# Cosformer attention and a token-mixing MLP on one core: tile-scheduled batches against a fixed order of head-pair slots

## The chip, the core and the metric

One NeuronCore of a Trainium2 chip runs the kernel; the other seven cores are idle. The metric is device time in microseconds. Before the change it was 181.37 us (median of three runs, 178.93 to 183.41). One more execution was profiled: its own time was 179.77 us, and its span from the first to the last recorded instruction 178.0 us.

## What is computed

There are 8 batches, 8 heads, 576 positions and 64 features a head. Float32 goes in and out; the kernel computes in bfloat16 with float32 sums.

```python
def phi(x, c, s):                      # c, s: cos and sin of pi/2 * pos/576
    r = np.maximum(x, 0.0)
    return np.concatenate([r * c, r * s], axis=-1)      # 64 -> 128 features
kv  = np.einsum('bhsf,bhsd->bhfd', phi(k), v)           # 128 x 64 for each head
z   = np.sum(phi(k), axis=2)
num = np.einsum('bhsf,bhfd->bhsd', phi(q), kv)
den = np.einsum('bhsf,bhf->bhs', phi(q), z)[..., None] + 1e-06
x   = num / den                                         # heads side by side: 576 x 512
W   = 1/8 * (x @ w_q) @ (x @ w_k).T                     # 576 x 576, never formed
out = np.maximum(W @ x, 0.0) @ w_out
```

Both kernels use W @ x = (x @ w_q) @ ((x @ w_k).T @ x): a 64 x 512 product "kx", then "mix" = relu(1/8 kx.T (x w_q).T), then mix times w_out.

## The kernel before, in words

The unit of work is a head pair: two heads, whose 2 x 576 x 64 values of q, k or v lie in memory as 128 partitions x 576 numbers. Partitions 0 to 63 hold the first head and 64 to 127 the second; 9 chunks of 64 features lie in each partition. Four pairs make a batch.

The loop at L278 goes over the batches. `attention` (L112) loads q, k and v on the SP queue in halves of a batch (quarters for batch 0). Relu of k and q (L140, ScalarE nearly always) goes to bfloat16, and VectorE multiplies each by a table of cos and sin (L142) into k_p and q_p, twice as wide. GpSimd casts v (L135) into a buffer in which each head has its own 65 columns (64 and a column of ones, for z) and zeros in the other head's columns, so that one 128-row matmul with 130 columns serves both heads. For each pair, TensorE forms kv_ps (L153, 9 matmuls) and transposes q_p (L163, 9); kv_ps and qpt_ps are copied to SBUF (L161, L167); then 5 matmuls a head give numerator and denominator (L175), and VectorE takes the reciprocal (L183) and multiplies (L184) into x_sb.

`moe_front` (L191) transposes x (L196, copied at L201), forms (x w_q).T and (x w_k).T in one product (L207, copied at L214), transposes the second back (L218, L225), forms kx (L229, L237) and mix (L242, L249). `wout` (L256) runs once for two batches: 9 row tiles of 4 matmuls (L260), a copy each (L268), two stores each on the SP queue (L276).

Nothing fixes the order by hand: the tile framework's scheduler interleaves the batches by dependencies and priorities, and `nc.any` lets it choose between VectorE and ScalarE. At the start 26 warming matmuls run (L60), tables and zeroed buffers are made, and the weights are loaded on ScalarE's queue.

PSUM has 8 banks: one each for kv_ps, 2 for qpt_ps, 2 for num_ps, 3 shared by everything of the mlp (tag "moe").

## Time and profile before

| | |
|---|---|
| runs: median (range) | 181.37 us (178.93 to 183.41) |
| profiled execution: its own time, its span | 179.77 us, 178.0 us |
| TensorE matmul busy in the span | 147.2 us (83%) |
| VectorE busy | 134.1 us (75%) |
| ScalarE, GpSimd busy | 89.9 us, 56.6 us |
| granted TensorE clock, mean | 0.932 |
| HBM read, written | 29.62 MB, 9.44 MB |

PE is TensorE, PEld its weight loads, DVE VectorE, ACT ScalarE, POOL GpSimd, SP the engine that issues transfers. A row "128x65 bf16 x320 | 21.3, 196" says 320 instructions of that shape, 21.3 us together, 196 ns of one on average. The end of a matmul is modelled and its time holds a fixed latency, so consecutive matmuls overlap in the records: what TensorE really spends on one is the spacing of starts in a run of equals.

### The profile page before, as it was taken

The page shows a single profiled execution, that of the slowest core. Times are in us where ns is not written, and L with a number is a line of the kernel's source. Part 1 is how long each engine was busy: PE and PEld are TensorE (multiplying, and loading weights), DVE is VectorE, ACT ScalarE, POOL GpSimd, SP SyncE. Part 2 cuts the span into 40 slices and gives each one's busy share as a digit, 9 for nine tenths or more (in the row PEclk, how much of TensorE's full clock was granted, in tenths as well). Part 3 has the DMA queues.
Part 4 walks back from the last instruction along what each step waited for, and adds up shares of the span by engine and source line. Part 5 has one row for each costly group of instructions (what it writes and reads, how often), then busy time and mean ns, then how long its engine had stood idle before and what let it go on. Part 6 is the DMA issues. An engine that isn't in the chain of part 4 may idle for free.

```text
span 178.0 us, 3706 instructions
## 1 busy us (share of the span) xinstructions
PE 147.2 (83%) x1434; PEld 90.6 (51%) x1434; DVE 134.1 (75%) x279; ACT 89.9 (51%) x167; POOL 56.6 (32%) x75
## 2 busy tenths in 40 slices
PE   6920776889958999999989999998999999759930
PEld 2300774656645446875745467675544756423410
DVE  5827989869999899897799999879994976722000
ACT  3028155148607869525496862491885426033630
POOL 8636283887882300000576000145800000000000
PEclk9995579579999999999999999999999999996996
DMA  6999999999792038789990587999008850000886
GB/s 172 312 393 315 382 397 392 391 392 388 256 387 109 2 80 186 166 220 398 397 385 37 130 204 170 292 400 389 19 0 195 205 135 0 4 0 0 189 201 140
DMA packets 20513, 39.30 MB, mean 221 GB/s; under 512 B 3088, under 2 KB 3088, under 8 KB 20496
## 3 DMA queue, kind: packets, MB, share of 16 engines
q1 hardware_dynamic: 18912, 37.76, 66.7%
q10 hardware_dynamic: 1584, 1.31, 2.5%
q8 instruction: 11, 0.18, 0.4%
q14 instruction: 6, 0.05, 0.1%
HBM read 29.62 MB, written 9.44 MB: 219 GB/s over the span
## 4 chain that ended last, share of the span: by engine, by line
PE 56%; DVE 17%; ACT 10%; DMA 8%; issue 4%; SPq 1%; POOL 0%; ACTq 0%
PE moe_ps_e L260 10%; PE kv_ps L153 10%; PE qpt_ps L163 9%; PE moe_ps_d L242 6%; PE moe_ps_c L229 5%; PE xT_ps L196 5%; PE num_ps L175 5%; DMA qf<-in_q_dram 5%; DVE k_p L142 5%; PE moe_ps_a L207 4%; DVE q_p L142 3%; DVE qpt_sb L167 3%; DVE x_sb L184 3%; ACT wqkT_sb L214 2%; DMA wq_f<-in_moe_w_q_dram 2%
## 5 line engine op out<-in xcount | busy, mean ns | idle before, releaser
L135 POOL CAST v_buf<-vf 64x576 bf16<-64x576 f32 x64 | 51.2, 822 | 71.9 <-DMA vf<-in_v_dram 33.4
L163 PE MATMUL qpt_ps<-ident,q_p 128*128 128x128 bf16 x288 | 29.8, 228 | 10.5 <-DVE q_p L142 9.4
L260 PE MATMUL moe_ps_e<-wo_sb,mix_sb 128*128 128x512 bf16 x144 | 33.9, 391 | 0.3
L153 PE MATMUL kv_ps<-v_buf,k_p 128*128 128x130 bf16 x288 | 29.0, 235 | 2.0 <-ACT kv_sb L161 0.8
L184 DVE TENSOR_TENSOR x_sb<-num_ps,rec 128x320 bf16<-128x320 f32 x64 | 29.8, 481 | 0.1
L167 DVE COPY qpt_sb<-qpt_ps 128x1152 bf16<-128x1152 bf16 x32 | 24.1, 754 | 4.7 <-PE qpt_ps L163 4.2
L268 ACT COPY o_sb<-moe_ps_e 128x512 f32<-128x512 f32 x34 | 19.9, 586 | 13.5 <-PE moe_ps_e L260 7.2
L163 PEld LDWEIGHTS <-q_p 128*128 128x128 bf16 x288 | 19.1, 102 | 14.9 <-DVE q_p L142 10.7
L175 PE MATMUL num_ps<-kv_sb,qpt_sb 128*128 128x65 bf16 x320 | 21.3, 196 | 3.0 <-DVE x_sb L184 1.5
L142 DVE TENSOR_TENSOR k_p<-rk,cossin 128x2304 bf16<-128x2304 bf16 (+1 forms) x18 | 23.3, 1297 | 0.2 <-ACT rk L140 0.2
L140 ACT ACTIVATE rk<-kf 128x1152 bf16<-128x1152 f32 (+1 forms) x17 | 17.7, 1048 | 11.1 <-DVE k_p L142 5.6
L142 DVE TENSOR_TENSOR q_p<-rq,cossin 128x2304 bf16<-128x2304 bf16 (+1 forms) x18 | 23.2, 1290 | 0.0
L260 PEld LDWEIGHTS <-mix_sb 128*128 128x128 bf16 x144 | 14.1, 100 | 17.0 <-issue 2.6
L153 PEld LDWEIGHTS <-k_p 128*128 128x128 bf16 x288 | 19.7, 105 | 5.3 <-ACT kv_sb L161 1.7
L249 ACT ACTIVATE mix_sb<-moe_ps_d 128x512 bf16<-128x512 f32 (+1 forms) x50 | 19.3, 441 | 5.1 <-PE moe_ps_d L242 4.7
L161 ACT CAST kv_sb<-kv_ps 128x130 bf16<-128x130 f32 x24 | 6.4, 268 | 28.0 <-PE kv_ps L153 28.0
L175 PEld LDWEIGHTS <-qpt_sb 128*128 128x128 bf16 x320 | 15.6, 99 | 9.4 <-issue 2.5
L140 ACT ACTIVATE rq<-qf 128x1152 bf16<-128x1152 f32 (+1 forms) x17 | 18.3, 1080 | 3.4 <-DMA qf<-in_q_dram 3.0
L196 PE MATMUL xT_ps<-ident,x_sb 128*128 128x128 bf16 (+1 forms) x160 | 17.4, 220 | 1.3 <-DVE x_sb L184 1.1
L242 PE MATMUL moe_ps_d<-wqkT_sb,kx_sb 64*128 64x512 bf16 x64 | 14.9, 288 | 1.1 <-ACT kx_sb L237 0.7
L201 DVE COPY xT_sb<-xT_ps 128x576 bf16<-128x576 bf16 x32 | 13.4, 441 | 2.4 <-PE xT_ps L196 2.2
L196 PEld LDWEIGHTS <-x_sb 128*128 128x128 bf16 (+1 forms) x160 | 11.6, 99 | 5.1 <-DVE x_sb L184 1.2
(45 smaller groups left out, 103.0 us busy)
## 6 DMA issues: line engine op xcount, KB each, us to landing
out_dram<-o_sb SPq DMA_DIRECT2D x72, 128.0 KB, 2.4
kf<-in_k_dram SPq DMA_DIRECT2D x14, 576.0 KB, 9.5
vf<-in_v_dram SPq DMA_DIRECT2D x14, 576.0 KB, 9.5
qf<-in_q_dram SPq DMA_DIRECT2D x14, 576.0 KB, 10.5
kf<-in_k_dram SPq DMA_DIRECT2D x4, 288.0 KB, 5.4
vf<-in_v_dram SPq DMA_DIRECT2D x4, 288.0 KB, 6.2
qf<-in_q_dram SPq DMA_DIRECT2D x4, 288.0 KB, 7.5
wo_f<-in_moe_w_out_dram ACTq DMA_DIRECT2D x1, 1024.0 KB, 10.7
```

The source lines that it names most:

```text
L135: nc.gpsimd.tensor_copy(v_ext[p0:p0 + 64, pr, :, hh, 0:D], dst[p0:p0 + 64, pr, :].rearrange("p (c d) -> p c d", c=C9))
L140: nc.any.tensor_scalar(rr[:, a:bb, :, :], dst[:, a:bb, :], 0.0, None, op0=ALU.max)
L142: nc.vector.tensor_mul(pp[:, a:bb, :, :, :], rr[:, a:bb, :, :].unsqueeze(3).to_broadcast([P, step, C9, 2, D]), csb)
L153: nc.tensor.matmul(kv_ps, k_p[:, pr, c, :, :], v_ext[:, pr, c, :, :], start=(c == 0), stop=(c == C9 - 1),)
L163: nc.tensor.transpose(qpt_ps[:, c, :], q_p[:, pr, c, :, :], ident)
L167: nc.vector.tensor_copy(qpt_sb, qpt_ps.rearrange("f c (hh pp) -> f hh c pp", hh=2))
L175: nc.tensor.matmul(num_ps[:, u, :], qpt_sb[:, hh, cb:cb + 2, :], kv_sb[:, hh, :], start=True, stop=True,)
L184: nc.vector.tensor_tensor(x_sb[:, :, h, :], num_ps[:, :, 0:D], rec.to_broadcast([P, SC, D]), op=ALU.mult,)
L196: nc.tensor.transpose(xT_ps[:, j0:j0 + npn], x_sb[p0:p0 + npn, u, 2 * hp:2 * hp + 2, :], ident[p0:p0 + npn, p0:p0 + npn],)
L242: nc.tensor.matmul(mx_ps[:, 0:nn], kx_sb[:, dmc * P:(dmc + 1) * P], wqkT_sb[0:64, n0:n0 + nn], start=True, stop=True,)
L260: nc.tensor.matmul(o_ps, mix_sb[:, dmc, rt * P:(rt + 1) * P], wo_sb[:, dmc, :], start=(dmc == 0), stop=(dmc == NDM - 1),)
L268: nc.any.tensor_copy(o_sb, o_ps)
```

## The change

The whole kernel function is rewritten. The order of the instructions of each engine is now the order of the program text (`manual_schedule`), and the work is cut into 32 slots, one for each head pair g. What is done in a slot:

- `qk_pe(g)`: k'v and the transposed q for one pair. Each head is now a matmul of its own on 64 rows, the two heads alternating; v needs no zero columns. q is only rectified and doubled beforehand (`dup_q`, GpSimd); cos and sin are multiplied in when VectorE evacuates the transposed q (`cst`). Both results share one two-bank tile with one buffer.
- `num(g-1)`: both heads of the pair before, with the 1e-06 added by a small matmul, one reciprocal and one multiplication for both heads, one two-bank buffer.
- Pieces of the mlp of past batches, by r = g mod 4: mix of two batches back (r = 0 and 1), w_out of three batches back, x transposes, x w_k and x w_q, kx. x w_k is computed with x as the stationary operand, so that it needs no transposing back; w_q is stored twice, so that mix's matmuls run on two halves of 64 rows. All these share one PSUM tag of two two-bank buffers, and ScalarE evacuates all of them.
- Preparation: GpSimd alone does relu of k, the cast of v and the doubled relu of q for a pair of head pairs (H), two H ahead; VectorE multiplies k by cos and sin for one H ahead in every odd slot. Loads come three H ahead, in pairs of head pairs.

What does not fit the slots comes after the last slot. The weights are loaded on the SP queue behind the first loads, and cast on ScalarE in slots 1 to 3; 16 warming matmuls are left.

The diff, cut to its core (all lines are of the new kernel):

```diff
+    inp = ctx.enter_context(tc.tile_pool(name="inp", bufs=4))
+    prep = ctx.enter_context(tc.tile_pool(name="prep", bufs=2))
...
+    ctx.enter_context(tc.manual_schedule())
+    def m2_tile(dtype, name):
+        return psum.tile([P, 2, 512 if dtype is FP32 else 1024], dtype,
+                         name=name, tag="m2", bufs=2)
...
+    def load(H, nsplit=1, names=("k", "q", "v")):
...
+                nc.sync.dma_start(raw[nm, H][:, lo:lo + step, :],
+                                  srcs[nm][b][:, h0 + lo:h0 + lo + step, :])
...
+    def relu_k(H, lo, hi, eng):
...
+            eng.tensor_scalar(o, raw["k", H][:, lo:hi, :], FMAX, 0.0,
+                              op0=ALU.min, op1=ALU.max)
+    def mul_k(H, lo, hi):
...
+        nc.vector.tensor_mul(
+            kp[H][:, lo:hi],
+            rks[H][:, lo:hi].unsqueeze(3).to_broadcast([P, n, C9, 2, D]),
+            cossin.unsqueeze(1).to_broadcast([P, n, C9, 2, D]))
+    def cast_v(H, lo, hi, eng):
...
+            eng.tensor_scalar(dst, src, 1.0, 1.0, op0=ALU.mult, op1=ALU.mult)
+    def dup_q(H, lo, hi, eng):
...
+            eng.tensor_scalar(dst, src, FMAX, 0.0, op0=ALU.min, op1=ALU.max)
+    def qk_pe(g):
+        H, i = divmod(g, 2)
+        qk_ps = psum.tile([P, 2, 2048], mybir.dt.uint8, name="qk_ps", bufs=1)
...
+        for c in range(C9):
+            for hh in range(2):
+                p0 = hh * 64
+                nc.tensor.matmul(
+                    kvp[:, hh, :], kp[H][p0:p0 + 64, i, c, :, :],
+                    v_bufs[H % 3][p0:p0 + 64, i, c, 0:D + 1],
+                    start=(c == 0), stop=(c == C9 - 1))
+        for c in range(C9):
+            for hh in range(2):
+                p0 = hh * 64
+                nc.tensor.transpose(
+                    qt[:, hh, c * D:(c + 1) * D],
+                    qd[H][p0:p0 + 64, i, c, :, :],
+                    ident[p0:p0 + 64, p0:p0 + 64])
...
+        nc.vector.tensor_copy(kv_sb, kvp)
+        nc.vector.tensor_mul(
+            qpt_bufs[g % 3][:, :, 1:SLOTS, :],
+            qt.rearrange("f h (c d) -> f h c d", c=C9),
+            cst.unsqueeze(1).to_broadcast([P, 2, C9, D]))
+    def num(g):
...
+        num_ps = psum.tile([P, 2, 512], FP32, name="num_ps", bufs=1)
...
+            for u in range(SC):
+                nc.tensor.matmul(
+                    nv[:, hh, u, :], qpt_bufs[g % 3][:, hh, 2 * u:2 * u + 2, :],
+                    kvs[g][:, hh, :], start=(u == 0), stop=False)
+            nc.tensor.matmul(nv[:, hh, :, D], ones_t, eps_t, start=False, stop=True)
+        nc.vector.reciprocal(rec, nv[:, :, :, D:D + 1])
+        nc.vector.tensor_tensor(
+            xs[b][:, :, 2 * pr:2 * pr + 2, :].rearrange("p u h d -> p h u d"),
+            nv[:, :, :, 0:D], rec.to_broadcast([P, 2, SC, D]), op=ALU.mult)
+    def xT(H, eng):
...
+    def wk_stage(b, eng):
...
+    def wq_stage(b, eng):
...
+    def kx_stage(b, eng):
...
+    def mx(b, st, eng):
...
+            nc.scalar.activation(dst, mx_ps[:, :, 0:hs], AF.Relu, scale=scale_moe)
+    def wout(bp, rt0, n, engs):
...
+            copy(engs[0], o_sb[:, 0:n, :], o_ps[:, 0:n, :])
...
+                nc.sync.dma_start(dst, o_sb[hi * 64:hi * 64 + 64, r, :])
+    A, V, G = nc.scalar, nc.vector, nc.gpsimd
+    load(1)
+    load_w()
+    for lo in range(2):
+        relu_k(0, lo, lo + 1, A)
+        cast_v(0, lo, lo + 1, G)
+        dup_q(0, lo, lo + 1, A if lo == 0 else G)
+        mul_k(0, lo, lo + 1)
+    load(2)
+    relu_k(1, 0, 2, G)
+    cast_v(1, 0, 2, G)
+    dup_q(1, 0, 2, G)
...
+    for g in range(NG):
+        Bc, r = divmod(g, NPAIR)
+        H = g // 2
+        if g % 2 == 0 and H + 3 < NB:
+            load(H + 3)
+        if r == 0 and Bc >= 2:
+            mx(Bc - 2, 0, A)
+        if r == 1 and Bc >= 2:
+            mx(Bc - 2, 2, A)
+        qk_pe(g)
+        if r == 0 and Bc >= 2:
+            mx(Bc - 2, 1, A)
+        if r == 1 and Bc >= 2:
+            mx(Bc - 2, 3, A)
+        if g >= 1:
+            num(g - 1)
+        if g % 2 == 1 and H + 1 < NB:
+            mul_k(H + 1, 0, 2)
...
+        if g % 2 == 0 and H + 2 < NB:
+            relu_k(H + 2, 0, 2, G)
+            cast_v(H + 2, 0, 2, G)
+            dup_q(H + 2, 0, 2, G)
+        if r == 0 and Bc >= 3:
+            wout(*wouts(Bc - 3)[0], (A,))
+        if r == 1:
+            if Bc >= 1:
+                xT(2 * (Bc - 1) + 1, A)
+            if Bc >= 3:
+                wout(*wouts(Bc - 3)[1], (A,))
+        if r == 2:
+            if Bc >= 1:
+                wk_stage(Bc - 1, A)
+                wq_stage(Bc - 1, A)
+            if Bc >= 3 and len(wouts(Bc - 3)) > 2:
+                wout(*wouts(Bc - 3)[2], (A,))
+        if r == 3:
+            if Bc >= 1:
+                kx_stage(Bc - 1, A)
+            xT(2 * Bc, A)
+    num(NG - 1)
+    for st in range(4):
+        mx(B - 2, st, A if st % 2 else V)
+    xT(2 * (B - 1) + 1, V)
+    for w in wouts(B - 3):
+        wout(*w, (A,))
+    wk_stage(B - 1, V)
+    wq_stage(B - 1, A)
+    for w in wouts(B - 2)[:1]:
+        wout(*w, (A,))
+    kx_stage(B - 1, V)
+    for w in wouts(B - 2)[1:]:
+        wout(*w, (A,))
+    for st in range(4):
+        mx(B - 1, st, A if st % 2 else V)
+    for w in wouts(B - 1):
+        wout(*w, (A, V))
```

`xT` makes 10 transposes of 128 x 128 and one copy of 128 x 1152; `wk_stage` 20 matmuls of 64 columns and a copy of 128 x 640; `wq_stage` 8 matmuls of 288 columns and a copy of 128 x 576; `kx_stage` 5 matmuls of 512 columns and a copy of 128 x 512; each `mx` 2 matmuls of 288 columns, each on 64 rows of its own, and a copy of 128 x 576; `wout` 4 matmuls of 512 columns for a row tile and one copy for two tiles. In this diff H counts pairs of head pairs (two slots), g head pairs, b batches; `wouts(b)` gives 2 or 3 groups of at most two row tiles.

More of the change, by code (lines that the diff above doesn't have):

```diff
@@ L56, with warm_up @@
+    load(0, nsplit=2)
     warm = consts.tile([P, 512], BF16)
     nc.vector.memset(warm, 1.0)
[L58 to L60 removed]
+    warm_ps = m2_tile(FP32, "warm_ps")
+    def warm_up(n):
+        for _ in range(n):
+            nc.tensor.matmul(warm_ps[:, 0, :], warm[:, 0:P], warm,
+                             start=True, stop=True)
+    warm_up(16)
@@ new lines, in xT, with copy @@
+    def xT(H, eng):
+        b, h = divmod(H, 2)
+        xT_ps = m2_tile(BF16, "xT_ps")
+        for i in range(2):
+            hp = 2 * h + i
+            for u in range(SC):
+                nc.tensor.transpose(
+                    xT_ps[:, i, u * P:(u + 1) * P],
+                    xs[b][:, u, 2 * hp:2 * hp + 2, :], ident)
+        copy(eng, xT_bufs[b % 2][:, 2 * h:2 * h + 2, D:SLOTS * D],
+             xT_ps[:, :, D:SLOTS * D])
+    def copy(eng, dst, src):
+        if eng is nc.scalar:
+            nc.scalar.copy(dst, src)
+        else:
+            eng.tensor_copy(dst, src)
@@ L256, in wout @@
-    def wout(b0, mix_sb):
-        for rt in range(2 * S // P):
-            o_ps = psum.tile([P, DM], FP32, name="moe_ps_e", tag="moe", bufs=3)
+                    wk_ps[:, 0, u * DH:(u + 1) * DH],
+                    xT_bufs[b % 2][:, dmc, u * P:(u + 1) * P],
+                    wk_sb[:, dmc, :], start=(dmc == 0), stop=(dmc == NDM - 1))
+        wkj = moe.tile([P, SC, 2, DH], BF16, name="wkj")
+        copy(eng, wkj, wk_ps[:, 0, 0:SC * DH].rearrange(
+            "p (u j) -> p u j", u=SC).unsqueeze(2).to_broadcast([P, SC, 2, DH]))
@@ L268, in wout @@
-            nc.any.tensor_copy(o_sb, o_ps)
+                    o_ps[:, r, :], mixs[bp][:, dmc, rt * P:(rt + 1) * P],
+                    wo_sb[:, dmc, :], start=(dmc == 0), stop=(dmc == NDM - 1))
+        if len(engs) == 1:
+            copy(engs[0], o_sb[:, 0:n, :], o_ps[:, 0:n, :])
+        else:
+            for r in range(n):
+                copy(engs[r], o_sb[:, r, :], o_ps[:, r, :])
+        for r in range(n):
             for hi in range(2):
-                bloc, j0 = divmod(128 * rt + 64 * hi, 576)
-                c = j0 // 64
+                bloc, j0 = divmod(P * (rt0 + r) + 64 * hi, S)
```

339 lines of the change are left out of this document (155 added, 184 removed).

## The prediction

> **What bounds the kernel now.** I read the windows by stage first, then the runs of equal matmuls on the timeline, then VectorE's groups.
>
> ```profile
> core 0 of [0], span 178.0 us
> 0.00:18.80 18.80, 8.60 (x26) 3.11 (x26) 12.11 (x18) 7.37 (x11) 11.27 (x19) 0.87 0.91 300
> 18.80:152.40 133.60, 123.61 (x1335) 81.11 (x1336) 117.23 (x250) 74.56 (x141) 45.38 (x56) 0.95 0.72 234
> 152.40:178.00 25.60, 15.04 (x77) 6.37 (x75) 4.78 (x14) 7.98 (x15) 0.00 (x0) 0.86 0.40 93
> ```
>
> The columns are time, then busy us of PE, PEld, DVE, ACT, POOL, then granted clock, DMA share and GB/s. Three stages: a head of 18.8 us without a useful matmul, 133.6 us for 32 head pairs (4.18 us each), a tail of 25.6 us after the last pair. Outside the span lie 179.77 - 178.0 = 1.8 us. In the middle PE is busy 93% and DVE 88%, ACT 56%, POOL 34%. PE's figure is flattering, because each record holds a latency; the spacing in runs of equals is the real price:
>
> ```profile
> 119.10 0.64 PE L153 MATMUL kv_ps<-v_buf,k_p 128*128 128x130 bf16 x8
> 119.57 0.61 PE L163 MATMUL qpt_ps<-ident,q_p 128*128 128x128 bf16 x8
> 111.47 0.31 PE L175 MATMUL num_ps<-kv_sb,qpt_sb 128*128 128x65 bf16 x5
> 111.88 0.32 PE L218 MATMUL moe_ps_b<-ident,wqkT_sb 64*128 64x64 bf16 x5
> 62.18 6.20 PE L260 MATMUL moe_ps_e<-wo_sb,mix_sb 128*128 128x512 bf16 x28
> 156.95 1.38 PE L229 MATMUL moe_ps_c<-x_sb,wkj_sb 128*64 128x512 bf16 x5 [0.42 <-DVE wkj_sb L225]
> 116.73 0.20 PE L242 MATMUL moe_ps_d<-wqkT_sb,kx_sb 64*128 64x64 bf16 x1
> 116.87 0.23 PE L163 MATMUL qpt_ps<-ident,q_p 128*128 128x128 bf16 x1
> ```
>
> Taking one latency (0.22 at 128 to 130 columns, 0.19 at 64 and 65, 0.38 at 512) off each and dividing by the rest gives 0.060 us for 130 columns, 0.056 for 128, 0.030 for 65, 0.032 for 64 and 0.216 for 512. The old pair costs PE 9 x 0.060 + 9 x 0.056 + 10 x 0.030 = 1.34 us, and the mlp a quarter of (18 + 4 + 4) x 0.216 + 1.38 + 16 x 0.056 + about 17 x 0.032 = 8.4 us, that is 2.1: 3.45 of 4.18 us. So PE is near its bound but loses 0.7 us a pair to hand-offs, and DVE, at 117.23 / 32 = 3.66 us, is as near. Both have to shrink for the middle to shrink.
>
> **The change, part by part: the head.** Before, the first transposes wait for DVE, which stood behind a weight cast and the tables:
>
> ```profile
> 4.01 0.68 ACT L140 ACTIVATE rk<-kf 128x576 bf16<-128x576 f32 x1 [0.39 <-DMA kf<-in_k_dram]
> 18.83 1.14 PE L163 MATMUL qpt_ps<-ident,q_p 128*128 128x128 bf16 x9 [8.77 <-DVE q_p L142]
> GB/s 172 312 393 315 382 397 392 391 392 388 256 387 109 2 80 186 166 220 398 397 385 37 130 204 170 292 400 389 19 0 195 205 135 0 4 0 0 189 201 140
> q10 hardware_dynamic: 1584, 1.31, 2.5%
> kf<-in_k_dram SPq DMA_DIRECT2D x14, 576.0 KB, 9.5
> ```
>
> Weight casts and the v memsets leave that path: the first k is there at 4.0, the tables by about 5 (an estimate), then one relu (0.68), one doubled q (1.16, L140 below) and one product (about 1.3) follow, so that the first slot can begin about 8 us in. But then transfers set the pace. A pair of pairs is 3 x 576 KB = 1.77 MB; the weights, moved to SP's queue behind load(1), are 1.31 MB (q10's bytes). The first two slices (4.45 us each) move 2.15 MB by 8.9 us; after that 0.393 MB/us. In the order of SP's queue v of H=1 lands at 8.9 + (3.54 - 2.15)/0.393 = 12.4 us, and k, q, v of H=2 at 17.3, 18.8 and 20.3. GpSimd then still casts v (1.2) and doubles q (2.4; its prices are below): slot 4 cannot start before 23.9 us. Slots 2 and 3 fit in front (v of H=1 cast by 13.7, q doubled by 16.1, then two slots). So the new head is "slot 4 at 23.9", which equals slot 0 at 8.7 if a slot takes 3.8.
>
> **TensorE per slot.** Matmuls on 64 rows of 64 or 65 columns replace those of 128 to 130: 18 x 0.030 + 18 x 0.032 = 1.12 us, if the two heads run one after the other; num 12 x 0.030 = 0.36. Changing between 64-row and 128-row matmuls costs about 0.1 (from 116.73 to 116.87 is 0.14, of which 0.03 to 0.04 are the 64 columns): twice a slot, 0.2; the mix pieces stand beside `qk_pe`, in the same form. The mlp of a batch: xT 20 x 0.056, wk 20 x 0.032, wq and mix 16 x 0.122 (0.216 x 288/512), kx 5 x 0.216 (before 1.38, with a 64-wide stationary operand), w_out 18 x 0.216: 8.7 us, 2.17 a slot. Sum 3.85 us if serial; if the heads run fully side by side, 0.56 + 0.12 less: 3.2. No row here shows two row halves together; the nearest, L218, is a single half. I take the middle, 3.5, and keep both ends.
> The Trainium skill, "TensorEngine Tiling (Array Packing)", section Key Properties, says that different tiles can load weights and multiply in parallel, and also that a change of tiling mode drains the engine. The first would give 3.2, the second is what the 0.1 us may be; neither enters the sum beyond that.
>
> **VectorE per slot.**
>
> ```profile
> L184 DVE TENSOR_TENSOR x_sb<-num_ps,rec 128x320 bf16<-128x320 f32 x64 | 29.8, 481 | 0.1
> L167 DVE COPY qpt_sb<-qpt_ps 128x1152 bf16<-128x1152 bf16 x32 | 24.1, 754 | 4.7 <-PE qpt_ps L163 4.2
> L142 DVE TENSOR_TENSOR q_p<-rq,cossin 128x2304 bf16<-128x2304 bf16 x14 | 19.5, 1393 | 0.0
> L201 DVE COPY xT_sb<-xT_ps 128x576 bf16<-128x576 bf16 x32 | 13.4, 441 | 2.4 <-PE xT_ps L196 2.2
> L183 DVE RECIPROCAL rec<-num_ps 128x5 f32<-128x5 f32 x64 | 10.5, 181 | 4.6 <-PE num_ps L175 4.3
> L161 DVE CAST kv_sb<-kv_ps 128x130 bf16<-128x130 f32 x8 | 2.4, 294 | 1.8 <-PE kv_ps L153 1.7
> 64.02 1.35 DVE L142 TENSOR_TENSOR q_p<-rq,cossin 128x2304 bf16<-128x2304 bf16 x1
> 65.29 1.35 DVE L142 TENSOR_TENSOR k_p<-rk,cossin 128x2304 bf16<-128x2304 bf16 x1
> ```
>
> Gone: the q multiplication (1.27 by spacing, one per two pairs) and the xT copies (0.44 a pair, to ACT). Kept or merged: kv_sb 0.29, reciprocal of 10 columns 0.2, multiplication of 640 elements 2 x 0.48 less one fixed part of 0.15 = 0.81, mul_k of two pairs 2 x 1.27 - 0.1 = 2.45 in odd slots. New: the evacuation of q becomes a product with `cst`. The nearest row is the copy of the same 1152 elements, 0.75; the other end is one element a cycle (L184: 0.333 us for 320 elements beyond its 0.15, so 1.20 + 0.15 = 1.35). I take 0.75. With 0.07 of overlap each: 1.8 + 1.22 = 3.0 us a slot, and waits for GpSimd's port (below) 0.3: 3.3.
> The Trainium skill, "VectorE: DVE Perf Modes", section on the perf-mode tier table, lists tensor_tensor with a PSUM operand at one element a cycle, which is the 1.35; its next section on PSUM operands allows twice that for 16-bit data, which is the 0.75. The copy cannot decide, and the first reading is a rival below.
>
> One buffer for qk_ps makes a loop over two slots: `qk_pe` of the odd slot, DVE's 0.75 + 0.9 + 2.45 + 0.6 of port wait, the next kv_sb and q product 1.0, then `qk_pe` again 0.85 and 0.4 of hand-offs: 7.0, that is 3.5 a slot.
>
> **GpSimd.** Relu of k (1152 elements), cast of v (1152) and doubled q (2304) for two slots all move here; ScalarE and DVE did the relus before.
>
> ```profile
> L135 POOL CAST v_buf<-vf x64: 657/682/1863, 6.2 to 128.5; 64x576 bf16<-64x576 f32 x64
> L104 POOL MEMSET v_buf<- x2: 2090/2136/2182, 1.5 to 3.6; 64x2340 bf16 x2
> 84.31 2.65 POOL L135 CAST v_buf<-vf 64x576 bf16<-64x576 f32 x4 [24.85 <-PE qpt_ps L163]
> 88.84 3.65 POOL L135 CAST v_buf<-vf 64x576 bf16<-64x576 f32 x4 [1.88 <-PE kv_ps L153]
> 89.61 1.71 DVE L142 TENSOR_TENSOR q_p<-rq,cossin 128x2304 bf16<-128x2304 bf16 x1
> ```
>
> The cast costs 657/576 = 1.14 ns an element with its fixed part, the memset 0.91: 4608 elements take 4.2 to 5.25 us. These are other instructions (tensor_scalar with two operations, no row), so the upper end is twice the cast, 10.5. I take 5.0, near the cast: 1.2, 1.2 and 2.4 with waits aside. The last three rows show that the two engines block each other: four casts take 2.65 us alone, and 3.65 beside a DVE product, which itself is stretched from 1.35 to 1.71. In the new order `dup_q` waits for the odd slot's transposes and so meets mul_k: up to 2.45 us are added, 7.45 for two slots, 3.7 a slot. mul_k in turn waits for the rest of a GpSimd instruction, on average some 0.6; behind it wait kv_sb and the q product, and TensorE for them.
>
> **ScalarE and SP.**
>
> ```profile
> L268 ACT COPY o_sb<-moe_ps_e 128x512 f32<-128x512 f32 x34 | 19.9, 586 | 13.5 <-PE moe_ps_e L260 7.2
> L140 ACT ACTIVATE rk<-kf 128x1152 bf16<-128x1152 f32 x13 | 15.0, 1162 | 5.6 <-DVE k_p L142 5.6
> L276 SPq DMA_DIRECT2D out_dram<-o_sb x72: 466/594/1888, 63.9 to 174.7; - x72
> L130 SPq DMA_DIRECT2D qf<-in_q_dram x18: 328/506/1532, 1.7 to 114.7; - x18
> HBM read 29.62 MB, written 9.44 MB: 219 GB/s over the span
> ```
>
> ACT evacuates the mlp: per batch mix 4 x 0.65, xT 2 x 1.16, wk 0.7, wq 0.65, kx 0.59, w_out 2.4: 9.3 us of a batch's 15. SP issues 9 stores x 0.594 + 6 loads x 0.506 = 8.4. All bytes at 0.393 MB/us take 99 us, 3.1 a slot. All three are hidden under 3.5 to 3.7; without that cover DMA would set 3.1.
>
> **Tail.** Left after slot 31: five row tiles, wk, wq, two, kx, two, mix, five: 14 x 0.864 + 0.64 + 0.98 + 1.08 + 0.98 + xT 0.56 + num and the two evacuations before it 1.9 = 18.2 us of PE; the last five tiles' ten stores then outlast PE, as nine tiles do now:
>
> ```profile
> 161.13 9.43 PE L260 MATMUL moe_ps_e<-wo_sb,mix_sb 128*128 128x512 bf16 x36
> 172.10 0.59 ACT L268 COPY o_sb<-moe_ps_e 128x512 f32<-128x512 f32 x1 [0.78 <-DMA out_dram<-o_sb]
> out_dram<-o_sb SPq DMA_DIRECT2D x72, 128.0 KB, 2.4
> ```
>
> Those five begin at 13.9; the first copy is done 2.4 later, ten issues take 6.2, the last landing 2.4: 25 us, about what the tail is now.
>
> **Sum.** 23.9 + 28 slots x 3.8 (GpSimd's 3.7, the largest, and 0.1 for hand-offs) = 130.3; + 25 = 155.3 of span, + 1.8 = **157 us**, against 179.77 of the profiled execution, which lies 0.9% below the median. The gain is 10 us in the head and 12 in the pace.
>
> **The rivals.**
> *Row halves run side by side and the port waits stay small* (each queue's wait is covered by slack): PE 3.2, loop 3.3, a slot 3.4; tail 24: 23.9 + 95.2 + 24 + 1.8 = 145. For it: nothing else on PE is long. Against: GpSimd's 3.7.
> *The q product runs at one element a cycle, or the fixed order loses what the scheduler found*: + 0.6 on DVE, twice in the loop: 8.3 for two slots, 4.2 a slot, the old pace. Then only the head is gained: 23.9 + 117.6 + 25 + 1.8 = 168. For it: L184 reads PSUM at that rate (in float32).
> *Slower: GpSimd bounds.* If its tensor_scalar costs 1.5 times the cast, 1.71 ns an element, two slots take 7.9 + 2.45 = 10.3, a slot 5.15, slot 4 starts at 26: 26 + 144 + 25 + 1.8 = 197. It decides from 1.45 ns an element (4.57 us a slot gives 180). For it: no row shows the instruction, and the doubled output. Against: the cast at 1.14 and the memset at 0.91.
> *The change does not do what it says* (the halves serial): PE 3.85, a slot 4.0, 23.9 + 112 + 25 + 1.8 = 163; it lies in the main case.
>
> **How the numbers follow.** Main case 0.50 (151 to 164), side by side 0.18, old pace 0.19, GpSimd 0.10, others 0.03. The range takes in the first three: 141 to 173. About 2% (177.7 and 185.0) is what a measurement can tell from no change. Faster: 0.50 + 0.18 + 0.18 = 0.86; slower 0.09, from GpSimd's case; same 0.05, between that and the old pace.
>
> **What would show it.** Right: slot 4's first k'v matmul near 24 us; 3.8 us between slots; GpSimd over 60% busy, its tensor_scalar of 1152 elements near 1.2 us; the q product near 0.75; a tail of 25. Wrong: a GpSimd row over 1.45 ns an element; the q product near 1.35; two row halves at 0.03 us a pair (then 145); or PE idle before `qk_pe` on DVE in every slot.

## The result and the profile after

The changed kernel takes 162.14 us (median of four, 161.92 to 162.92), the kernel before 181.28 us beside it (178.93 to 183.41): a ratio of 0.902, 95% interval 0.893 to 0.911. The forecast was 157, range 141 to 173. Repeated executions of one kernel fall into a faster and a slower state: medians and ranges are of all executions, ratios and their intervals of the faster ones alone. The profiled execution took 162.92 us, with a span of 161.1; again 1.8 us lie outside.

The windows of the changed kernel, cut where the prediction cut them: until slot 4 starts, 28 slots, tail (columns as before).

```profile
0.00:23.80 23.80, 12.36 (x206) 8.25 (x206) 17.32 (x27) 8.52 (x12) 13.78 (x29) 0.78 0.96 353
23.80:131.70 107.90, 88.58 (x1851) 61.36 (x1851) 75.96 (x125) 52.97 (x70) 61.18 (x40) 0.92 0.73 252
131.70:161.10 29.40, 18.50 (x129) 8.96 (x127) 7.64 (x11) 10.80 (x15) 0.00 (x0) 0.95 0.55 127
```

23.8 + 107.9 + 29.4 + 1.8 = 162.9 stands against the forecast's 23.9 + 106.4 + 25 + 1.8 = 157.1. A slot takes 107.9 / 28 = 3.85 us; PE is busy in 82% of that stage, where it was 93% before, so PE no longer sets the pace. GpSimd, which was to set it, is busy 61.18 of 107.9, or 57%.

The costliest groups on the page, chosen to answer the prices of the prediction:

```profile
L211 POOL TENSOR_SCALAR qd<-qf 128x2304 bf16<-128x2304 f32 (+1 forms) x16 | 33.7, 2109 | 10.2 <-issue 8.6
L223 PE MATMUL qk_ps<-v_buf,kp 64*128 64x65 bf16 x576 | 15.9, 201 | 25.1 <-DVE kp L187 21.3
...
L187 DVE TENSOR_TENSOR kp<-rk,cossin 128x2304 bf16<-128x2304 bf16 (+1 forms) x17 | 29.4, 1727 | 2.2 <-ACT rk L178 2.2
...
L198 POOL TENSOR_SCALAR v_buf<-vf 128x1152 bf16<-128x1152 f32 (+1 forms) x17 | 20.8, 1222 | 15.8 <-DMA vf<-in_v_dram 15.0
...
L180 POOL TENSOR_SCALAR rk<-kf 128x1152 bf16<-128x1152 f32 x15 | 17.7, 1180 | 16.0 <-DVE kp L187 10.3
L237 DVE TENSOR_TENSOR qpt_buf<-qk_ps,cst 128x1152 bf16<-128x1152 bf16 x32 | 23.9, 748 | 0.0
```

The second row says what held TensorE: the k'v matmuls were preceded by 25.1 us of idle TensorE, and 21.3 of these were ended by `kp`, the product of k with cos and sin (`mul_k`, L187). GpSimd's row L198 shows it idle for 15.8 us, nearly all of it for the loads of v, and its row L180 for 16.0 us, 10.3 of them for that product. The waits, with times and the longest:

```profile
PE qk_ps L223 <- DVE kp L187: 21.3, 14, 3.7
...
PE qk_ps L223 <- DVE qpt_buf L237: 3.6, 4, 2.6
```

One of the 14, on the timeline: an odd slot (k'v at 66.61) and the even one behind it.

```profile
66.61 0.46 PE L223 MATMUL qk_ps<-v_buf,kp 64*128 64x65 bf16 x18
...
68.50 0.82 DVE L256 TENSOR_TENSOR x_sb<-num_ps,rec 128x640 bf16<-128x640 f32 x1
...
69.24 1.57 DVE L187 TENSOR_TENSOR kp<-rk,cossin 128x2304 bf16<-128x2304 bf16 x1
...
70.86 0.46 PE L223 MATMUL qk_ps<-v_buf,kp 64*128 64x65 bf16 x18 [0.95 <-DVE kp L187]
...
71.16 0.42 PE L230 MATMUL qk_ps<-ident,qd 64*128 64x64 bf16 x18
...
71.42 0.29 PE L323 MATMUL mx_ps<-wqT,kx 64*128 64x288 bf16 x2
...
73.96 0.45 PE L223 MATMUL qk_ps<-v_buf,kp 64*128 64x65 bf16 x18
```

The program puts `mul_k` for the next two pairs at the end of the odd slot, behind that slot's evacuations on VectorE, and the first matmul that reads it is the first of the next slot. So TensorE finishes the odd slot's work inside the 1.57 us of product, is idle for the last 0.95, and starts the even slot at 70.86, 0.05 us after the product's end. From the odd slot to the even one it is 4.25 us, VectorE's chain with the product at its end; from the even one to the next, 3.10 us. Over slots 4 to 31 the two ways average 4.63 and 3.22 us. The first is longer than in this pair where GpSimd's `dup_q` has more of its time left when the product begins:

```profile
83.74 2.11 POOL L211 TENSOR_SCALAR qd<-qf 128x2304 bf16<-128x2304 f32 x1
...
84.35 2.71 DVE L187 TENSOR_TENSOR kp<-rk,cossin 128x2304 bf16<-128x2304 bf16 x1
```

Here the product took 2.71 us, where one without a GpSimd instruction beside it takes 1.35 (124.91).

### The profile page after: what moved, and what is told of

Same layout as the page of the kernel before. It is cut to its first block, busy times and chain, and to the rows that moved or that the text cites. A ratio compares the mean times of both kernels' runs of the same rounds, so it can differ in the third digit from the quotient of the medians.

```text
span 161.1 us, 5016 instructions
## 1 busy us (share of the span) xinstructions
PE 119.4 (74%) x2184; PEld 78.6 (49%) x2184; DVE 100.9 (63%) x163; ACT 72.3 (45%) x96; POOL 75.0 (47%) x68
## 4 chain that ended last, share of the span: by engine, by line
PE 42%; DVE 29%; ACT 7%; DMA 6%; SPq 5%; POOL 3%; issue 3%; ACTq 0%; POOLq 0%
DVE kp L187 14%; PE o_ps L341 14%; DVE x_sb L256 7%; PE qk_ps L223 6%; PE wq_ps L296 6%; DMA kf<-in_k_dram 6%; ACT o_sb L274 5%; PE num_ps L250 5%; PE qk_ps L230 4%; DVE qpt_buf L237 4%; PE wk_ps L282 4%; SPq L81 3%; PE mx_ps L323 2%; POOL qd L211 2%; DVE kv_sb L235 2%
## 5 line engine op out<-in xcount | busy, mean ns | idle before, releaser
L211 POOL TENSOR_SCALAR qd<-qf 128x2304 bf16<-128x2304 f32 (+1 forms) x16 | 33.7, 2109 | 10.2 <-issue 8.6
L223 PE MATMUL qk_ps<-v_buf,kp 64*128 64x65 bf16 x576 | 15.9, 201 | 25.1 <-DVE kp L187 21.3
L341 PE MATMUL o_ps<-wo_sb,mix_sb 128*128 128x512 bf16 x144 | 33.7, 379 | 0.1
L187 DVE TENSOR_TENSOR kp<-rk,cossin 128x2304 bf16<-128x2304 bf16 (+1 forms) x17 | 29.4, 1727 | 2.2 <-ACT rk L178 2.2
L223 PEld LDWEIGHTS <-kp 64*128 64x128 bf16 x576 | 12.3, 100 | 33.2 <-DVE kp L187 26.4
L198 POOL TENSOR_SCALAR v_buf<-vf 128x1152 bf16<-128x1152 f32 (+1 forms) x17 | 20.8, 1222 | 15.8 <-DMA vf<-in_v_dram 15.0
L256 DVE TENSOR_TENSOR x_sb<-num_ps,rec 128x640 bf16<-128x640 f32 x32 | 26.4, 825 | 1.1
L274 ACT COPY o_sb<-o_ps 128x1024 f32<-128x1024 f32 (+1 forms) x20 | 17.6, 885 | 20.7 <-PE o_ps L341 20.7
L180 POOL TENSOR_SCALAR rk<-kf 128x1152 bf16<-128x1152 f32 x15 | 17.7, 1180 | 16.0 <-DVE kp L187 10.3
L237 DVE TENSOR_TENSOR qpt_buf<-qk_ps,cst 128x1152 bf16<-128x1152 bf16 x32 | 23.9, 748 | 0.0
L330 ACT ACTIVATE mix_sb<-mx_ps 128x576 bf16<-128x576 f32 x28 | 17.7, 654 | 6.7 <-PE mx_ps L323 6.6
L250 PE MATMUL num_ps<-kv_sb,qpt_buf 128*128 128x65 bf16 x320 | 17.9, 204 | 0.1
```

The source lines that it names most:

```text
L180: eng.tensor_scalar(o, raw["k", H][:, lo:hi, :], FMAX, 0.0, op0=ALU.min, op1=ALU.max)
L187: nc.vector.tensor_mul(kp[H][:, lo:hi], rks[H][:, lo:hi].unsqueeze(3).to_broadcast([P, n, C9, 2, D]), cossin.unsqueeze(1).to_broadcast([P, ...
L198: eng.tensor_scalar(dst, src, 1.0, 1.0, op0=ALU.mult, op1=ALU.mult)
L211: eng.tensor_scalar(dst, src, FMAX, 0.0, op0=ALU.min, op1=ALU.max)
L223: nc.tensor.matmul(kvp[:, hh, :], kp[H][p0:p0 + 64, i, c, :, :], v_bufs[H % 3][p0:p0 + 64, i, c, 0:D + 1], start=(c == 0), stop=(c == C9 - 1))
L237: nc.vector.tensor_mul(qpt_bufs[g % 3][:, :, 1:SLOTS, :], qt.rearrange("f h (c d) -> f h c d", c=C9), cst.unsqueeze(1).to_broadcast([P, 2, ...
```

## The experiments

Each kernel is the changed one with the edit shown, timed beside the kernel before; the ratio is against that.

| kernel | median us (range) | ratio, 95% interval |
|---|---|---|
| mulk_early | 153.65 (151.58 to 155.21) | 0.844, 0.834 to 0.855 |
| heads_serial | 168.14 (166.87 to 169.35) | 0.932, 0.923 to 0.941 |
| dup_split | 161.69 (159.93 to 162.78) | 0.893, 0.880 to 0.906 |
| pool_more | 158.58 (156.28 to 160.31) | 0.876, 0.856 to 0.897 |
| weights_late | 161.94 (161.78 to 162.00) | 0.895, 0.889 to 0.901 |
| warm_slots | 162.16 (160.49 to 163.87) | 0.888, 0.880 to 0.896 |
| tail_av | 165.26 (164.70 to 165.78) | 0.916, 0.909 to 0.922 |
| tail_alt | 164.95 (164.09 to 165.24) | 0.911, 0.905 to 0.917 |
| tail_bufs | 162.16 (160.83 to 163.30) | 0.901, 0.885 to 0.916 |
| early_tail | 152.32 (149.79 to 154.64) | 0.839, 0.821 to 0.857 |
| early_tail_warm | 146.12 (145.60 to 147.30) | 0.815, 0.805 to 0.824 |
| early_whole | 270.92 (270.24 to 272.52) | 1.506, 1.498 to 1.513 |

The first theory was that the place of the product sets the pace; its rivals were GpSimd, the port that GpSimd shares with VectorE, and TensorE itself.

**mulk_early: the product one slot earlier.**

```diff
-        if g % 2 == 1 and H + 1 < NB:
+        if g % 2 == 0 and H + 1 < NB:
             mul_k(H + 1, 0, 2)
```

> The product of k with cos and sin for the next two pairs is issued in the even slot instead of the odd one, directly before which it is needed; nothing else is touched. Theory 1 (the pace is set by this late product): TensorE's waits for kp, 21.3 us in 14 waits in the changed kernel's profile, nearly vanish, and 12 to 16 us go: 146 to 150 us against 162.1. Rival 2 (GpSimd sets the pace, as the prediction had it): GpSimd's work is the same, so 161 to 163. Rival 3 (the wait only changes its name, to the one buffer of qk_ps behind VectorE's chain): PE then waits for qpt_buf instead, and 158 to 162 is measured.

It is the largest single step, 8.5 us by the medians (about 10 by the ratios), short of the 12 to 16 that were expected. Slot 4 starts at 22.39 instead of 23.82 and slot 31 at 117.61 instead of 128.99: 3.53 us from slot to slot instead of 3.90. In the changed kernel weight loads waited 26.4 us for the product, matmuls 21.3 and GpSimd 10.3. In the product's own view of this run, little of that is left:

```profile
L187 DVE TENSOR_TENSOR kp<-rk,cossin x17: 757/1359/3120, 7.5 to 110.1; 128x2304 bf16<-128x2304 bf16 x15, 128x1152 bf16<-128x1152 bf16 x2
...
who waited for it (us, times):
  PEld L223: 1.7, 2
  PE qk_ps L223: 0.8, 1
```

and in its waits the next one shows:

```profile
PE qk_ps L223 <- DVE qpt_buf L237: 5.8, 5, 2.0
```

21.3 us of waiting gave 11.3 us of span (161.1 to 149.8): with the product out of the way, the single `qk_ps` buffer, which is free only when the q product has read it, holds TensorE more often than before (5.8 instead of 3.6). The products for two pairs are about as long as before, 1707 ns on average instead of 1801, so that their place made the difference and not their length. The place of the product was the cause; how much it hid was overestimated.

**heads_serial: one head after the other.**

```diff
-        for c in range(C9):
-            for hh in range(2):
+        for hh in range(2):
+            for c in range(C9):
```

(in both loops of `qk_pe`)

> In k'v and in the transposes of q all nine matmuls of the first head come before the nine of the second, instead of alternating; same instructions. If the two row halves run side by side only when they alternate, the 18 k'v matmuls grow from 0.46 to about 0.54 us and the 18 transposes from 0.26 to about 0.58 (18 times 0.030 and 0.032). Theory 1 (qk_pe lies on the chain that sets the pace): 0.4 us for 32 slots, 172 to 176 us. Rival (PE has slack there): within 2 us of 162. Third case: spacing unchanged, then alternation is not what makes them overlap.

6 us slower, about half of what was expected. A slot of it on the timeline, nine matmuls of each head:

```profile
72.98 0.54 PE L223 MATMUL qk_ps<-v_buf,kp 64*128 64x65 bf16 x15 [0.95 <-DVE kp L187]
...
73.34 0.20 PE L230 MATMUL qk_ps<-ident,qd 64*128 64x64 bf16 x1
...
73.67 0.29 PE L323 MATMUL mx_ps<-wqT,kx 64*128 64x288 bf16 x1
```

The same view, cut after the first 0.15 us, has the first head's half alone:

```profile
72.98 0.33 PE L223 MATMUL qk_ps<-v_buf,kp 64*128 64x65 bf16 x5 [0.95 <-DVE kp L187]
```

One half alone takes (0.33 - 0.19) / 4 = 0.035 us a matmul here (0.032 in the prediction's row L218, of a single half). In the changed kernel's timeline above, 18 alternating matmuls take (0.46 - 0.19) / 17 = 0.016 each, 0.032 for a pair: two row halves do run side by side, in the time of one. In heads_serial the first 15 take (0.54 - 0.19) / 14 = 0.025 on average, so the second head's matmuls already run beside the first's among them; the transposes of the first head begin at 73.34, while k'v of the second is still running. So its `qk_pe` lasts 0.69 us (72.98 to 73.67) and not 1.12, against 0.56 (70.86 to 71.42) in the changed kernel. The halves overlap even where the program doesn't alternate them, but less. VectorE's evacuation begins 0.99 us after this slot's start instead of 0.76 (at 73.97, in the changed kernel at 71.62), and this slot and the next come 4.47 and 3.33 us after the one before them instead of 4.25 and 3.10: TensorE's own work at the start of a slot lies on the chain too.

**dup_split and pool_more: GpSimd and the port.** dup_split divides the longest GpSimd instruction, so that the product has to wait for less of it. pool_more gives GpSimd more to do: a memset of a tile that nobody reads.

```diff
-            dup_q(H + 2, 0, 2, G)
+            dup_q(H + 2, 0, 1, G)
+            dup_q(H + 2, 1, 2, G)
```

> GpSimd's doubled q is issued as two instructions of one pair each instead of one of two pairs. Theory 1 (VectorE's product waits for the end of the GpSimd instruction in progress, and that wait is on the chain): the longest products, 2.46 to 2.73 us against 1.35 undisturbed, shorten to 2.3 at most, and 2 to 4 us go: 158 to 160. Rival (GpSimd is the bound): its own work grows by 0.19 us for two slots, so 164 to 166. Rival (the stretch is hidden): 161 to 163.

```diff
             dup_q(H + 2, 0, 2, G)
+            idle_t = prep.tile([P, 2304], BF16, name="idle_t")
+            nc.gpsimd.memset(idle_t, 0.0)
```

> GpSimd gets one more instruction for every two slots, a memset of 2304 bfloat16 elements that nobody reads (about 2.1 us, 14 of them, 29 us in all). It writes only. As the prediction had it (GpSimd sets the pace with 7.45 us of 7.6 for two slots): 1 us a slot more, 188 to 192 us. Theory now (GpSimd has 4.4 us of work in 7.8 and waits for the rest): 162 to 165; its busy time rises from 75 to about 104 us. If its writes also held up VectorE's product, the products would become longer than in the changed kernel, 1.80 us on average.

The split shortens the mean product from 1727 to 1498 ns and the waits for it from 21.3 to 15.7 us, but its time can't be told from the changed kernel's. pool_more went against both theories: GpSimd worked more and the kernel got, if anything, faster. Its page, whose execution took 160.31:

```profile
PE 118.7 (75%) x2184; PEld 78.1 (49%) x2184; DVE 96.2 (61%) x163; ACT 72.2 (46%) x96; POOL 109.4 (69%) x82
L187 DVE TENSOR_TENSOR kp<-rk,cossin 128x2304 bf16<-128x2304 bf16 (+1 forms) x17 | 25.2, 1482 | 2.1 <-ACT rk L178 2.1
```

GpSimd goes from 75.0 to 109.4 us of work, so it did not set the pace. The memsets shift its reading instructions away from the products, which become shorter (1482 instead of 1727 ns). Eight of the products lay partly beside a memset and took 1.35 us each, one of them here:

```profile
54.50 2.02 POOL L405 MEMSET idle_t<- 128x2304 bf16 x1
...
55.50 1.35 DVE L187 TENSOR_TENSOR kp<-rk,cossin 128x2304 bf16<-128x2304 bf16 x1
```

That the memsets themselves don't stretch the product agrees with the Trainium skill, "SBUF — State Buffer", section Who interferes with whom: a VectorE instruction with two SBUF inputs collides with a GpSimd instruction that reads SBUF, not with one that only writes it. In their profiled executions both gain in the slots: slot 31 starts at 125.50 in dup_split and at 126.35 in pool_more, instead of 128.99. dup_split then loses 1.7 us in the tail, where the granted clock is 0.61 from 131.4 to 135.4 us. Whether that also lies behind the medians, 161.69 and 158.58, stays open.

**weights_late and warm_slots: the head.** The first puts the weights' loads behind one more pair of pairs, to see if transfers set slot 4. The second puts six matmuls with an unread result into each of slots 0 to 3, to see what the low clock there costs.

```diff
     load(1)
-    load_w()
...
     load(2)
+    load_w()
```

> The three weight loads are issued on SP behind the loads of the third pair of head pairs (load(2)) instead of ahead of them; the casts stay where they are. Theory (transfers set the pace of the head, as the prediction had it: q and v of H=2 wait behind 1.31 MB of weights): slot 4 starts about 3 us earlier than 23.8, and 2 to 3 us go: 159 to 160. Rival (VectorE's late product and the four slots themselves, 8.2 + 4 times 3.8 = 23.4, set slot 4 anyway): slot 4 within 1 us of 23.8, 161 to 163.

```diff
         qk_pe(g)
+        if g < 4:
+            warm_ps = m2_tile(FP32, "warm_ps")
+            for _ in range(6):
+                nc.tensor.matmul(warm_ps[:, 0, :], warm[:, 0:P], warm,
+                                 start=True, stop=True)
```

> Six more warming matmuls stand behind the transposes of each of the slots 0 to 3, where TensorE is idle; their result is not read. Theory (the granted clock of 0.5 to 0.6 between 20 and 45 us costs time, since matmuls of slots 4 to 9 take up to twice as long): the clock stays near 1.0 from 10 us on and slot 10 starts 3 to 5 us earlier than at 48.1; 157 to 160. Rival (in these slots VectorE and GpSimd set the pace and the slow matmuls are hidden, or the clock falls again after slot 4): 161 to 164.

Neither moves the median. In the changed kernel's timeline, the end of the head reads:

```profile
21.39 1.15 POOL L198 TENSOR_SCALAR v_buf<-vf 128x1152 bf16<-128x1152 f32 x1 [1.50 <-DMA vf<-in_v_dram]
...
22.41 1.35 DVE L187 TENSOR_TENSOR kp<-rk,cossin 128x2304 bf16<-128x2304 bf16 x1
...
22.62 3.11 POOL L211 TENSOR_SCALAR qd<-qf 128x2304 bf16<-128x2304 f32 x1
...
23.82 0.46 PE L223 MATMUL qk_ps<-v_buf,kp 64*128 64x65 bf16 x18 [1.73 <-DVE kp L187]
...
25.78 0.66 PE L230 MATMUL qk_ps<-ident,qd 64*128 64x64 bf16 x18 [1.50 <-POOL qd L211]
```

and with the weights late:

```profile
19.42 2.11 POOL L211 TENSOR_SCALAR qd<-qf 128x2304 bf16<-128x2304 f32 x1
...
21.82 1.35 DVE L187 TENSOR_TENSOR kp<-rk,cossin 128x2304 bf16<-128x2304 bf16 x1
...
23.23 0.68 PE L223 MATMUL qk_ps<-v_buf,kp 64*128 64x65 bf16 x18 [1.52 <-DVE kp L187]
```

GpSimd had its data 3.2 us earlier (`dup_q` at 19.42 instead of 22.62), slot 4 came only 0.6 us earlier: its first matmuls wait for the product in both. Its transposes, though, waited 1.50 us for `dup_q` in the changed kernel (last row) and not here, and slot 5 starts at 25.44 instead of 27.50, slot 16 at 69.09 instead of 70.86. So by these two traces the late data cost some 2 us in the first slots. In this execution the tail lost as much again: its first 20 w_out matmuls met a granted clock of 0.59 (132.0 to 136.2 us),

```profile
132.76 6.12 PE L341 MATMUL o_ps<-wo_sb,mix_sb 128*128 128x512 bf16 x20
```

against 4.48 us for the same 20 in the changed kernel, at a clock of 1.00. Whether the other executions lost the gain in this way isn't shown. The rows at 19.42 and 22.62 also show the port: `dup_q` takes 2.11 us alone and 3.11 where the product began before it. The clock by slices, changed kernel and warm_slots:

```profile
PEclk9995586556995999999999999999999999999996
```

```profile
PEclk9999997559869999999999999999999999999995
```

From 12 to 40 us the clock was mostly 0.5 or 0.6 in the changed kernel. The warming holds it at 0.9 or more up to 24 us and leaves three such slices behind that: from slot 4 to slot 10 it is 0.70, where it was 0.72. Slot 4 starts 2.2 us later than in the changed kernel (25.99), since the product began behind `dup_q` and took 3.05 us, and slot 10 at 48.12 us in both. So this run raised the clock only ahead of the slots in question, and what the low clock costs there isn't shown.

**tail_av, tail_alt, tail_bufs: the end.** The tail is 4.4 us longer than forecast. Three edits of what follows slot 31: both engines evacuate each group of w_out (tail_av), they take whole groups in turn (tail_alt), or the two banks each of `qk_ps` and `num_ps` serve as third and fourth buffer (tail_bufs).

```diff
-        wout(*w, (A,))
+        wout(*w, (A, V))
```

> After the last slot every group of output row tiles is evacuated by ScalarE and VectorE, one tile each, instead of by ScalarE alone. Theory (the tail of 29 us instead of the predicted 25 is TensorE waiting for evacuations of 1.02 us with two buffers, at 139.5, 144.2 and 147.2 us): 2 to 3 us go: 159 to 160. Rival (the stores' issue on SP, 32 in 31 us, ends the kernel whatever the evacuation does): 161 to 163.

```diff
-    for w in wouts(B - 3):
-        wout(*w, (A,))
+    for j, w in enumerate(wouts(B - 3)):
+        wout(*w, (V,) if j % 2 else (A,))
...
-        wout(*w, (A, V))
+        wout(*w, (V,) if j % 2 else (A,))
```

> After the last slot the groups of output row tiles are evacuated alternately by ScalarE and by VectorE, a whole group each, and never one group by both. Theory (with both engines on one tile the second copy waited for the first, 0.59 + 0.69 us instead of 1.02, which is why the split made the tail longer; evacuation is what TensorE waits for there): 2 to 3 us go, 159 to 160. Rival (stores on SP end the kernel): 161 to 163. If it is slower, VectorE's dearer copy (0.69 against 0.59 for 512 columns) costs more than the overlap gives.

```diff
     num(NG - 1)
+    tags += ["m2", "qk", "m2", "num"] * 8
```

(`m2_tile` takes the next of these tags while there are some)

> After the last num, the mlp's tiles take turns through four two-bank buffers instead of two: the two of the mlp and the banks of qk_ps and num_ps, which are free by then. Who evacuates is left as in the changed kernel. Theory (TensorE's 22.3 us in the tail against the 18.2 that were summed are waits for a buffer two tiles back, 0.5 to 1.0 us each at mix, wk and the second w_out): TensorE's part of the tail falls to 19 us and 3 to 4 us go: 158 to 159.5. Rival (the 28 stores on SP end the kernel): 161 to 163.

The first two are slower by 3 us in the medians, though their intervals touch that of the changed kernel; the third has the same median. In tail_av VectorE's copy waits for ScalarE's copy into the same tile, so that the two take 1.27 us in turn where ScalarE alone took 1.01 (at 147.24 below):

```profile
136.48 0.58 ACT L274 COPY o_sb<-o_ps 128x512 f32<-128x512 f32 x1 [2.57 <-PE o_ps L341]
...
137.10 0.69 DVE L276 COPY o_sb<-o_ps 128x512 f32<-128x512 f32 x1 [1.56 <-ACT o_sb L274]
```

In that execution TensorE's last 20 matmuls also met a granted clock of 0.72 and took 6.16 us instead of 4.49. In tail_alt the first copy of the last five tiles takes two tiles at once, and their stores begin 3.0 us after their first matmul (150.74 to 153.76) instead of 2.6. Neither adds up to 3 us, and the rest was not taken apart.

The changed kernel's tail, with its store issues seen in two windows, up to 151.5 and from 152 us:

```profile
138.76 12.24 SPq L355 DMA_DIRECT2D out_dram<-o_sb  x18
...
147.24 1.01 ACT L274 COPY o_sb<-o_ps 128x1024 f32<-128x1024 f32 x1 [2.02 <-PE o_ps L341]
...
149.57 4.49 PE L341 MATMUL o_ps<-wo_sb,mix_sb 128*128 128x512 bf16 x20
...
151.56 0.59 ACT L274 COPY o_sb<-o_ps 128x512 f32<-128x512 f32 x1 [1.23 <-PE o_ps L341]
...
152.17 6.24 SPq L355 DMA_DIRECT2D out_dram<-o_sb  x10
```

The 18 stores of the first nine tiles are all issued by 151.0. SP then stands idle for 1.2 us until the first copy of the last five tiles is done (152.15), and their ten stores take 6.24 us. So it is TensorE, coming to these tiles only at 149.57, that sets the end, and the stores are 1.2 us behind it. With tail_bufs this turns round:

```profile
141.88 16.81 SPq L359 DMA_DIRECT2D out_dram<-o_sb  x24
...
147.87 1.01 ACT L278 COPY o_sb<-o_ps 128x1024 f32<-128x1024 f32 x1 [1.69 <-DMA out_dram<-o_sb]
```

TensorE's tail falls from 22.3 us (131.75 to 154.06) to 20.2 (133.48 to 153.65). Now the stores run through without a pause for data, ScalarE's copy at 147.87 waits for one of them to free its tile (its matmuls ended at 146.96), and the last ten stores begin 0.65 us after their first copy is done. From the start of the last numerator to the end of the last issue it takes 25.2 us instead of 26.7. But the slots of that execution ended 1.7 us later, at a mean clock of 0.880 instead of 0.906, and the median shows no gain. Stores that follow one another without a pause are issued 0.64 us apart, and the kernel before ended in such a run too:

```profile
163.69 11.60 SPq L276 DMA_DIRECT2D out_dram<-o_sb  x18
```

**early_tail and early_tail_warm: what works, together.** early_tail is mulk_early with tail_bufs; early_tail_warm adds warm_slots and weights_late.

> The earlier product of k and the four buffers in the tail together. If both causes are independent, 153.7 less 3: 150 to 151. If the tail's gain was already in part that of the stores, 152 to 154.

> The same with the six warming matmuls in slots 0 to 3 and the weights loaded behind load(2). Alone these two gave nothing while VectorE's late product set the pace. With the product early, TensorE itself is nearer the bound, and a clock of 0.55 between 24 and 32 us should cost something: 1 to 3 us less than early_tail if so; no difference if the early slots are still paced by VectorE and GpSimd.

tail_bufs adds nothing that can be told beside mulk_early (0.839, interval 0.821 to 0.857, against 0.844). The edits of the head, without effect on the median alone, take it to 146.12 us, the fastest kernel here. The windows of early_tail_warm, cut at 22 and at 116.5 us:

```profile
0.00:22.00 22.00, 16.61 (x230) 8.70 (x230) 14.44 (x23) 5.68 (x10) 14.80 (x29) 1.00 0.95 342
22.00:116.50 94.50, 84.83 (x1841) 59.57 (x1842) 76.50 (x130) 54.61 (x72) 67.92 (x39) 0.96 0.84 296
116.50:143.80 27.30, 18.68 (x139) 9.55 (x136) 8.13 (x12) 10.91 (x15) 0.00 (x0) 0.94 0.61 143
```

From slot 4 (23.48) to slot 31 (114.47) a slot takes 3.37 us; TensorE is busy 90% again. Why it gains is not shown. In the profiled executions slot 10 starts at 43.50 us in early_tail and at 43.11 here, so the head itself gave 0.4 us; slots 10 to 31 take 73.9 and 71.4 us at a clock of 1.00 in both, so the clock isn't the reason there either. Which of the two head edits counts was not taken apart.

**early_whole: half as many issues.** If SP's issues set the tail, one store of 128 rows for each tile should shorten it.

```diff
             for hi in range(2):
...
-                    ap=[[C9 * DM, 64], [1, DM]])
-                nc.sync.dma_start(dst, o_sb[hi * 64:hi * 64 + 64, r, :])
+            dst = dataclasses.replace(
+                out, offset=out.offset + at[0],
+                ap=[[at[1] - at[0], 2], [C9 * DM, 64], [1, DM]])
+            nc.sync.dma_start(dst, o_sb[:, r, :])
```

> On top of early_tail_warm, each row tile of the output is stored by one transfer of 128 rows instead of two of 64, all through the kernel: 36 issues on SP instead of 72. Theory (the tail is set by SP: in the changed kernel 28 stores follow one another from 138.8 to 157.8 us, 0.65 us apart, whoever evacuates, which is why tail_av, tail_alt and tail_bufs gained nothing): TensorE's last matmul, at 136.7 in early_tail_warm, sets the end instead, plus a copy of 0.6, an issue of 0.6 and a landing of 2.4 to 2.7: the span falls from 143.8 to 140.5 to 141, 142 to 143.5 us in all against 146.1. Rival (an issue of twice the rows takes twice as long): 146.

It takes 271 us, and says nothing on the question, since a store of this shape is slow by itself. Its issues and a window late in the run (DMA share and GB/s are the last two columns):

```profile
199.74 30.86 SPq L361 DMA_DIRECT2D out_dram<-o_sb  x6
```

```profile
200.00:260.00 60.00, 11.73 (x39) 4.11 (x37) 3.59 (x5) 4.94 (x7) 0.00 (x0) 0.61 0.13 51
```

A store of 256 KB takes 5.1 us, at 51 GB/s and 0.13 of the 16 DMA engines' time, and ScalarE waits for its tiles. 0.13 is 2 of 16. The Trainium skill, "DMA: Bandwidth & Descriptors", section Why a DMA increments its semaphore by 16 and not by 1, has the rule: the number of engines is the largest one up to 16 that divides the slowest dimension of both sides. Here these are 2 and 128, which makes 2 engines; the trace agrees. With 64 rows as the slowest dimension, as in all other kernels here, it is 16. So what sets the 0.64 us between two stores, SP's issue or the transfers, stays open: while the stores of tail_bufs run (144.0 to 158.7 us), the DMA engines are busy for 0.85 of the time. Stores from a second queue were not tried.

## Why the prediction was right or wrong

The time lies within the range and 3% above the forecast, and the way to it was partly wrong. That the head and the pace came out at their numbers is luck.

*Head, slot 4 at 23.9: it came at 23.82, for another reason.* The failed step is "transfers set the pace", which holds for half of the slot. Its k'v was released by the product, and weights_late moved it by only 0.6. Its transposes did wait for `dup_q` behind the late data, up to 25.78 us, and weights_late brought slot 5 forward by 2.1.

*Pace, 3.8 a slot: 3.85 measured, wrong engine.* "GpSimd's 3.7, the largest" failed. Its three instructions cost 1.15, 1.15 and 2.11 us alone, 4.4 for two slots instead of 5.0, and the port adds little instead of the 2.45 assumed: `dup_q` took 33.7 us where 15 x 2.11 + 1.15 would be 32.8. It was busy 57% of the slots, 47% of the span, and not the "over 60%" looked for; and with 34 us more of work the kernel was not slower. The wait that did set the pace was in the prediction's loop over two slots, which had DVE's product between the odd slot's evacuations and the next `qk_pe`; but it was priced at 3.5 a slot and dropped for being smaller than 3.7. It should have been asked for each operand how long before its use it is made: here 0.05 us.

*mul_k, "2 x 1.27 - 0.1 = 2.45": mis-sized.* The count was wrong. The old instruction of 2304 numbers already holds two pairs, doubled, and so does the new one: 1.35 us alone (22.41 above). The port's 0.6 was near: the 15 full products average 1.80 us, 0.45 above that. This error hid a second one. With 1.35 the loop would have come to 5.9 for two slots, against 7.8 measured (4.63 + 3.22). Its sum names `qk_pe` of both slots and holds one 0.85. And it priced the way from the even slot to the odd one at 1.0 + 0.85 + 0.4 = 2.25 us, VectorE and `qk_pe` alone, while TensorE's mlp pieces stand in that slot and make it 3.22.

*TensorE 3.5, between 3.2 and 3.85: the lower end was true.* The halves run side by side (0.032 a pair; 0.56 for `qk_pe` to the next matmul). The rival built on that gave 145 us, and it needed "loop 3.3"; in this kernel the late product stood in the way. With the product moved, the head warmed, the weights late and four buffers in the tail, 146.1 us came out, at 3.37 a slot. The Trainium skill's rule that different tiles can load and multiply in parallel ("TensorEngine Tiling (Array Packing)", Key Properties) agrees with the 0.032 us. Two of the signs that the prediction named for being wrong thus came: a pair at 0.03 us, and PE idle before `qk_pe` on DVE, the second in 12 of the 14 even slots from slot 4 on.

*q product 0.75: right, 748 ns.* Of the two sections of the Trainium skill's "VectorE: DVE Perf Modes", the one on why PSUM operands drop a tier (up to two elements a cycle for 16 bit) agrees with the trace; the tier table's row for tensor_tensor, which would give about 1.35 us by the prediction's estimate, does not, and the measurement decides.

*ScalarE, SP and DMA hidden: right in the slots.* In the 28 slots their busy shares are 49% (ScalarE) and 0.73 (DMA).

*Tail 25: 29.4.* The failed step is "Those five begin at 13.9": TensorE came to the last five tiles 17.9 us after the last slot (149.57 - 131.70). The 18.2 us are matmuls alone, and TensorE's waits for evacuations, 3.8 us ahead of these tiles in the trace, were put at nothing. From there on the forecast held: the first copy done 2.6 us later (2.4 forecast), ten issues of 6.2, 2.4 to land; 1.0 more lies between the last landing and the end of the span. A second limit was overlooked, though it cost nothing yet: the other nine tiles' 18 stores stand in front of these ten, and at 0.64 us each they left SP only 1.2 us of slack. Two more buffers took 2.1 us off TensorE's part, and the stores then set the end.

*The slower rival, GpSimd at over 1.45 ns an element,* fell with 0.92 to 1.0 ns.

## What to carry to other kernels

In an order written by hand, look for each operand at the time between the end of its making and its first use: a product that stands last in the slot before its use can leave TensorE idle for most of its length (0.95 of 1.57 us in the pair shown), though no engine is full, and moving one line was worth more than any other single edit here. Price the tail by each engine and queue by itself, the issuing queue too, and give an engine its waits for evacuation and not its matmuls alone. Edits that showed nothing are worth another try after the largest wait is gone: some of them gained here together with the moved product, for a reason that stays open. And compare two traces stage by stage, since a stretch of low clock in one of them can hide what an edit gained.
